# Packed attention and a gated feed-forward layer in one kernel: the first batch written out in another order

## The chip, the cores and the metric

The kernel runs on 1 core of one Trainium2 chip. The metric is the device time of one execution in microseconds (us); lower is better. The engines are TensorE (PE for its matmuls, PEld for its weight loads), VectorE (DVE), ScalarE (ACT), GpSimd (POOL) and SyncE (SP), which issues nearly all DMA transfers.

## The reference, cut to what matters

Eight batches of 8 heads, 576 tokens and head dimension 64. In each head 32 packed queries `p` attend to `k` and `v`; what comes out serves as key and as value for an attention from `q`. The heads are laid side by side (512 wide) and go through a feed-forward layer with 2048 hidden columns. The weights are float64 in memory.

```python
def _attn_ref(q, k, v, p):
    ...
    p_packed = sm_attn(p, k, v)                 # 32 rows a head
    out = sm_attn(q, p_packed, p_packed)        # 576 rows a head
    return out.astype(np.float32)

def _moe_ref(x, w_in, w_out):
    h = x @ w_in                                # 512 -> 2048
    g = h * (1.0 / (1.0 + np.exp(-1.702 * h)))
    return (g @ w_out).astype(np.float32)       # 2048 -> 512
```

## The kernel before

All work is cut into small steps, each a Python function that issues a few instructions. A tuple called `order` lists 2856 steps in the sequence in which they are issued, and the schedule is manual: every engine, and every DMA queue, executes its own instructions strictly in the order in which the tuple issues them. The tuple therefore sets the order of every queue. A step's last argument may name the engine that does it (`dve`, `pool`); without one it takes the step's default.

The steps of one batch `b`, with the names that the profile shows:

- `load` issues the input transfers on SP: `k` (with `p` in front, tile `k`, in two parts), `v` (a large part 0 of 1024 KB, `v_last` as part 1 of 256 KB) and `q` in two parts. The three share two buffers, so `q` takes the buffer of `k`, and the next batch's `k` that of `v`.
- `scores1_first` / `scores1_mm` (L250) multiply packed queries with keys. In batch 0 `max1_first` (DVE L273), `bias1` (DVE L303) and `exp1_first` (ACT L314) follow, and `turn1_mm` (PE L345), `turn1_copy`, `turn1_last_copy` (ACT L364) bring the weights transposed into the tile `aT`. `pack` (PE L408) multiplies `aT` with `v`; `pack_end` (ACT L421), `pack_turn_mm` (PE L427) and `pack_turn_copy` give `PT`, the packed rows.
- In the other batches `exp1` (ACT L321) and `turn1_blocks` (DVE L376) take the place of the PE transposes. They write the tile `xb` (0 and 1 for the even and odd heads); eight transfers `turn1_out` (SP L384, `aside<-xb`) carry it to DRAM, and six `turn1_in` (SP L396, `aT<-aside`) bring it back into `aT`.
- `scores2_mm` (PE L495) multiplies `q` with `PT`. Then `scores2_turn` (DVE L506), `max2` (DVE L526), `sub2` (L530), `exp2` (ACT L534), `sum2` (DVE L539 to L541), `norm2` (POOL L545), `turn2` (DVE L551).
- Every large product works on values split into an upper and a lower part, which are multiplied as three matmuls. `a_upper`/`a_lower` split the attention weights, `m_upper`/`m_lower` (L471) the product `m` of `PT` with `w_in` that `m_chunk` (PE L437) makes 512 hidden columns at a time, `h_upper`/`h_lower` (L592) the gated values `ghi`/`glo`, `upper_w`/`lower_w` (L232) the weights `wo`. The upper part is a cast (L117 on ACT, L119 on DVE or POOL), the lower one a subtraction.
- `h_mm` (PE L605) makes 128 hidden columns of one half of the tokens, six matmuls. It writes one of two PSUM banks, so it must wait until the `h_mm` two before it has gone through `h_tanh` (ACT L613) and `h_gate`/`h_over` (DVE L595).
- `out_mm` (PE L665) adds 128 hidden columns to the output of 128 tokens, three matmuls of 128x512.
- In batch 0 the weights come in too. `load_w` (SP L189) brings tile number `n` of 32: 0 to 3 are `w_in` for the first 512 hidden columns, 4 to 7 four tiles of `w_out`, 8 to 11 `w_in` again, and so on. The tiles 0 to 3 are loaded and decoded in two halves of 256 columns. `begin_w` (ACT L208, `tops<-raw`) and `join_w` (DVE L220) decode the float64 words. Tiles 16 to 19 must be joined before `w_out` tiles 20 to 23 can be loaded, because these use the same memory.
- `warm` (PE L125) is a run of matmuls whose result nobody reads.

The casts that name no engine go to ACT, the subtractions that name none to POOL:

```python
    def upper_w(n, engine=nc.scalar):
    ...
    def h_upper(b, f, half, engine=nc.scalar):
    def h_lower(b, f, half, engine=nc.gpsimd):
```

Work of neighbouring batches is interleaved: while batch 0 is in its feed-forward layer, the keys, scores and transposes of batch 1 run in between.

Of the kernel before, what the change touches and what calls it, by code (L numbers as in the profile page):

```python
# [21 lines left out]
def kernel(  # L22
# [681 lines left out]
    early = [bank_acc(0), bank_acc(1)]  # L704
    late = [bank_acc(2), bank_acc(3)]
    inner = [bank_h, bank_h]
# [9 lines left out]
        (turn1_last_copy, 0), (sum1, 0, 1), (pack, 0, 0, late), (pack, 0, 1), (pack_end, 0),
        (pack_turn_mm, 0), (warm, 5, 2), (pack_turn_copy, 0, dve), (load_w, 2, 0), (begin_w, 2, 0),
        (join_w, 2, 0), (load, "q", 0, 0), (load, "q", 0, 1), (scores2_mm, 0, 0),
        (scores2_turn, 0, 0, 0), (scores2_turn, 0, 0, 1), (max2, 0, 0, 0), (max2, 0, 0, 1),
        (load_w, 3, 0), (begin_w, 3, 0), (warm, 6, 2), (sub2, 0, 0, 0, pool), (exp2, 0, 0, 0),  # L720
        (scores2_mm, 0, 1, late), (scores2_turn, 0, 1, 1), (scores2_turn, 0, 1, 0), (max2, 0, 1),
        (load_w, 1, 0), (warm, 9, 3), (warm, 10, 3), (join_w, 3, 0), (begin_w, 1, 0),
        (join_w, 1, 0), (sub2, 0, 0, 1, pool), (m_chunk, 0, 0, early, 0), (exp2, 0, 0, 1),
        (load_w, 0, 1), (begin_w, 0, 1), (sum2, 0, 0, 0), (norm2, 0, 0, 0, pool), (warm, 2, 3),
        (m_upper, 0, 0, 1, 0), (sub2, 0, 1, None), (exp2, 0, 1), (sum2, 0, 0, 1),
        (norm2, 0, 0, 1, pool), (sum2, 0, 1), (warm, 0, 3), (load_w, 3, 1), (begin_w, 3, 1),
        (join_w, 3, 1), (load, "k", 1, 0), (scores1_mm, 1, 0, inner), (turn2, 0, 0, 0),
        (turn2, 0, 0, 1), (scores1_copy, 1, 0, 1), (scores1_copy, 1, 0, 0), (warm, 3, 3),
        (m_upper, 0, 0, 0, 0), (m_lower, 0, 0, 0, 0), (load_w, 4), (begin_w, 4), (join_w, 4),
        (m_lower, 0, 0, 1, 0), (a_upper, 0, 0, 0), (a_upper, 0, 0, 1), (join_w, 0, 1),  # L730
        (load_w, 2, 1), (begin_w, 2, 1), (norm2, 0, 1, None, pool), (a_lower_mm, 0, 0, 0, bank_b),
        (a_lower_mm, 0, 0, 1, bank_b), (a_lower_copy, 0, 0, 1, dve), (turn2, 0, 1),
        (a_lower_copy, 0, 0, 0), (upper_w, 4), (join_w, 2, 1), (load_w, 1, 1), (begin_w, 1, 1),
        (join_w, 1, 1), (h_mm, 0, 0, 0), (h_tanh, 0, 0, 0), (h_gate, 0, 0, 0), (lower_w, 4),
        (load, "k", 1, 1), (a_upper, 0, 1, None), (a_lower, 0, 1),
        (scores1_mm, 1, 1, (bank_b, bank_b)), (scores1_copy, 1, 1, 0), (scores1_copy, 1, 1, 1),
        (scores1_max, 1, 0), (h_mm, 0, 1, 0), (h_tanh, 0, 1, 0), (h_gate, 0, 1, 0),
        (h_upper, 0, 0, 0), (h_lower, 0, 0, 0), (m_chunk, 0, 0, (bank_b, bank_b), 1),
        (m_upper, 0, 0, 0, 1, dve), (load_w, 5), (bias1, 1, 0), (begin_w, 5), (join_w, 5),
# [12 lines left out]
        (h_mm, 0, 3, 1), (h_tanh, 0, 3, 1), (h_over, 0, 3), (m_chunk, 0, 1), (h_gate, 0, 3, 1),
        (m_upper, 0, 1, 0, None), (m_lower, 0, 1, 0), (m_upper, 0, 1, 1, None), (m_lower, 0, 1, 1),
        (h_mm, 0, 3, 0), (h_tanh, 0, 3, 0), (h_gate, 0, 3, 0), (h_upper, 0, 3, 0, dve),
        (out_mm, 0, 1, 1), (load_w, 12), (load_w, 13), (scores1_max, 1, 1), (bias1, 1, 1),
        (load_w, 19), (begin_w, 12), (join_w, 12), (exp1, 1, 0), (lower_w, 6), (out_mm, 0, 2, 0),
        (h_lower, 0, 2, 1), (load_w, 14), (out_mm, 0, 2, 1), (h_upper, 0, 3, 1, dve),
# [12 lines left out]
        (h_mm, 0, 6, 0), (begin_w, 18), (h_tanh, 0, 6, 0), (h_gate, 0, 6, 0), (upper_w, 15),  # L770
        (lower_w, 15, dve), (out_mm, 0, 4, 1), (out_mm, 0, 5, 1), (turn1_out, 1, 1, 3),
        (begin_w, 17), (upper_w, 14), (join_w, 18), (join_w, 17), (turn1_out, 1, 1, 2),
        (h_mm, 0, 7, 1), (h_tanh, 0, 7, 1), (begin_w, 19), (join_w, 19), (out_mm, 0, 4, 2),
        (out_mm, 0, 5, 2), (h_over, 0, 7), (lower_w, 14, dve), (h_mm, 0, 7, 0), (h_tanh, 0, 7, 0),
        (h_gate, 0, 7, 0), (m_chunk, 0, 2), (h_gate, 0, 7, 1), (h_upper, 0, 6, 0),
# [6 lines left out]
        (load, "v", 1, 0), (upper_w, 21, dve), (join_w, 20), (upper_w, 20, dve),
        (lower_w, 21, dve), (h_upper, 0, 6, 1), (out_mm, 0, 6, 1), (h_lower, 0, 7, 1),
        (out_mm, 0, 7, 1), (h_mm, 0, 8, 0), (h_tanh, 0, 8, 0), (h_gate, 0, 8, 0),
        (h_lower, 0, 6, 1), (h_mm, 0, 8, 1), (turn1_in, 1, 1), (h_upper, 0, 8, 0),
# [659 lines left out]
```

## Time and profile before

| | before |
|---|---|
| median of 3 runs | 698.79 us (697.97 to 699.39) |
| the profiled execution | 699.15 us, span 697.4 us |
| PE busy | 685.8 us (98%) |
| DVE, ACT, POOL busy | 439.1, 258.3, 95.9 us |
| mean granted TensorE clock | 0.999 |
| first `h_mm` starts | 25.01 us |
| `pack` of batch 1 starts | 72.49 us |

Times inside the execution count from the start of the span. "Idle before, releaser" on a row is the time for which its engine waited just before it, and what let it go. Matmuls overlap, so the start of a matmul says more than its end.

### The profile page before, as it was taken

To read this page: it belongs to the slowest core of one execution; us is meant where nothing else is said; L and a number is where in the kernel's file an instruction comes from. 1 tells how busy PE (TensorE), PEld (TensorE's weight loads), DVE (VectorE), ACT (ScalarE), POOL (GpSimd) and SP (SyncE) were. 2 spreads that over 40 slices of the span, in tenths; PEclk is the share of its full clock that TensorE was granted. 3 is DMA by queue.
4 is the path that set the end of the run, shared out by engine and by line. 5 is a ranking of instruction groups with operands and counts; after the bars stand their busy time and mean duration, and the time that the engine had idled before them with its cause. 6 is when DMAs were issued, how large, how long until landed. Compare 5 with 4: busy or idle time off the path is not lost.

```text
span 697.4 us, 12984 instructions
## 1 busy us (share of the span) xinstructions
PE 685.8 (98%) x5030; PEld 560.8 (80%) x5030; DVE 439.1 (63%) x1111; ACT 258.3 (37%) x620; POOL 95.9 (14%) x115
## 2 busy tenths in 40 slices
PE   7999999999999999999999999999999999999997
PEld 5788688888888888887888878888888887878885
DVE  4987885537555467555685567775785647855453
ACT  3886544423324323433223233332232333333220
POOL 2553372122300224111000000000000000000000
PEclk9999999999999999999999999999999999999999
DMA  9989803342101612055000613034200160010001
GB/s 331 378 306 223 299 0 106 70 136 77 65 0 20 194 31 87 16 130 184 1 31 1 159 43 144 16 93 127 96 16 1 31 181 1 16 47 1 1 15 61
DMA packets 55260, 65.18 MB, mean 93 GB/s; under 512 B 35808, under 2 KB 40864, under 8 KB 54176
## 3 DMA queue, kind: packets, MB, share of 16 engines
q1 hardware_dynamic: 55120, 64.23, 29.1%
q8 instruction: 40, 0.66, 0.4%
q14 instruction: 20, 0.16, 0.1%
q10 hardware_dynamic: 80, 0.13, 0.0%
HBM read 50.78 MB, written 13.57 MB: 92 GB/s over the span
## 4 chain that ended last, share of the span: by engine, by line
PE 92%; DMA 4%; issue 1%; DVE 1%; SPq 1%; ACT 0%; DVEq 0%; ACTq 0%
PE acc L665 49%; PE h L605 28%; PE acc_over L665 5%; PE psm_None L437 4%; PE ps L495 1%; PE pspv L408 1%; PE ps L250 1%; DMA aT<-aside 1%; DMA q<-q 1%; DMA k<-pk 1%; DMA aside<-xb 1%; SPq L384 1%; SPq L396 0%; SPq L189 0%; DVE ghi L119 0%
## 5 line engine op out<-in xcount | busy, mean ns | idle before, releaser
L665 PE MATMUL acc<-wo,ghi 128*128 128x512 f32 x1024 | 322.9, 396 | 0.4 <-ACT ghi L117 0.4
L665 PEld LDWEIGHTS acc<-wo,ghi 128*128 128x128 f32 x1024 | 179.6, 188 | 41.0 <-issue 11.2
L613 ACT ACTIVATE g<-h 128x288 f32<-128x288 f32 x256 | 104.0, 410 | 276.8 <-PE h L605 261.3
L665 PE MATMUL acc<-wo,glo 128*128 128x512 f32 x512 | 201.9, 394 | 0.3 <-POOL glo L592 0.3
L595 DVE SCALAR_TENSOR_TENSOR g<-g,h 128x288 f32<-128x288 f32 (+1 forms) x256 | 104.9, 415 | 116.2 <-ACT g L613 115.6
L605 PE MATMUL h<-ahi,mhi 128*128 128x288 f32 x496 | 139.9, 297 | 0.3 <-DVE g L595 0.3
L605 PE MATMUL h<-ahi,mlo 128*128 128x288 f32 x496 | 138.7, 295 | 0.0
L665 PEld LDWEIGHTS acc<-wo,glo 128*128 128x128 f32 x512 | 96.1, 188 | 23.6 <-POOL glo L592 0.9
L605 PEld LDWEIGHTS h<-ahi,mhi 128*128 128x128 f32 x496 | 93.2, 188 | 16.3 <-DVE x L506 4.9
L605 PE MATMUL h<-alo,mhi 128*128 128x288 f32 x496 | 104.9, 292 | 0.0
L605 PEld LDWEIGHTS h<-ahi,mlo 128*128 128x128 f32 x496 | 93.4, 188 | 6.9
L592 DVE TENSOR_TENSOR glo<-g,ghi 128x224 fp32r<-128x224 f32 (+1 forms) x183 | 76.2, 427 | 14.8 <-ACT ghi L117 10.8
L592 POOL TENSOR_TENSOR glo<-g,ghi 128x224 fp32r<-128x224 f32 (+1 forms) x73 | 55.4, 765 | 193.3 <-DVE ghi L119 86.7
L605 PEld LDWEIGHTS h<-alo,mhi 128*128 128x128 f32 x496 | 79.7, 188 | 0.1
L117 ACT CAST ghi<-g 128x288 fp32r<-128x288 f32 (+1 forms) x142 | 55.2, 403 | 54.4 <-DVE g L595 47.7
L595 DVE SCALAR_TENSOR_TENSOR over<-g,h 128x64 f32<-128x64 f32 x128 | 27.0, 214 | 30.6 <-ACT g L613 30.1
L471 DVE TENSOR_TENSOR mlo<-psm_None,mhi 128x512 fp32r<-128x512 f32 x60 | 40.6, 684 | 5.1 <-ACT mhi L117 4.9
L119 DVE CAST ghi<-g 128x224 fp32r<-128x224 f32 (+1 forms) x114 | 35.9, 320 | 7.0 <-PE acc L665 1.4
L665 PE MATMUL acc_over<-wo,ghi_over 128*128 128x512 f32 x128 | 39.8, 392 | 0.0
L117 ACT CAST mhi<-psm_None 128x512 fp32r<-128x512 f32 x45 | 26.2, 584 | 29.3 <-PE psm_None L437 29.3
L437 PE MATMUL psm_None<-w_in,PT 64*32 64x512 f32 x496 | 33.4, 596 | 0.0
L665 PEld LDWEIGHTS acc_over<-wo,ghi_over 128*128 128x128 f32 x128 | 23.6, 188 | 4.8
(95 smaller groups left out, 476.1 us busy)
## 6 DMA issues: line engine op xcount, KB each, us to landing
q<-q SPq DMA_DIRECT2D x16, 576.0 KB, 5.7
v<-v SPq DMA_DIRECT2D x8, 1024.0 KB, 5.4
o<-o SPq DMA_DIRECT2D x32, 256.0 KB, 2.8
raw<-w_out SPq DMA_DIRECT2D x16, 511.8 KB, 7.2
raw<-w_in SPq DMA_DIRECT2D x12, 511.8 KB, 8.9
k<-pk SPq DMA_DIRECT2D x8, 640.0 KB, 4.0
k<-pk SPq DMA_DIRECT2D x8, 576.0 KB, 6.7
aside<-xb SPq DMA_DIRECT2D x56, 72.0 KB, 2.3
```

Of the source, the lines that this page charges most:

```text
L117: nc.scalar.copy(dst, src)
L119: engine.tensor_copy(dst, src)
L250: nc.tensor.matmul(bank[32 * j : 32 * j + 32, :NH], kq["p", b][rows(eo), j, :], kq["k", b][rows(eo), half, j, :], start=True, stop=True,)
L384: nc.sync.dma_start(d[:, :, NP * eo + j, :], src.rearrange("t (g n) -> t g n", n=NPK))
L408: nc.tensor.matmul(bank[32 * j : 32 * j + 32, e * D : (e + 1) * D], aT[:, c, e, 32 * j : 32 * j + 32], vt[:, c, e0 : e0 + D], start=(c == ...
L437: nc.tensor.matmul(banks[eo][32 * j : 32 * j + 32, columns(part)], PT[rows(eo), j, :], w_in_sb[fc][rows(eo), j, columns(part)], start=True ...
L471: nc.vector.tensor_tensor(lo, bank[:, at], hi.bitcast(F32), op=ALU.subtract)
L592: engine.tensor_tensor(lo, src, hi.bitcast(F32), op=ALU.subtract)
L595: nc.vector.scalar_tensor_tensor(dst, th, 1.0, h, op0=ALU.add, op1=ALU.mult)
L605: nc.tensor.matmul(h[:, :NH], m[eo][part][:, fo : fo + P], a[:, eo * NH : (eo + 1) * NH], start=(n == 0), stop=(n == len(terms) - 1),)
L613: nc.scalar.activation(g, st["h", b, f, half][:, :NH], AF.Tanh, scale=1.702)
L665: nc.tensor.matmul(acc, gp[:, at : at + P], wo[f][:, part, :], start=(start and i == 0), stop=(stop and i == 2),)
```

## The change

Only the tuple `order` changes. It holds the same 2856 steps, and from its step 331 on (a little before the second half of batch 0's `h_mm`s) it is the same as before. The first 330 steps stand in another sequence, and 30 of them name another engine. There are as many `warm` steps as before.

Casts and copies that go from DVE to ACT: `turn1_copy` of batch 0 (two), `pack_turn_copy`, `a_lower_copy` (one), `m_upper` (one), `h_upper` for hidden tile 3 (two) and 5 (one), `upper_w` 6 and 21. From ACT to DVE: `a_upper` (one), `h_upper` for tiles 0 (two), 1, 2, 4 and 7 (one each), `upper_w` 7, 12, 14 and 15. From DVE to POOL: `sub2` of the second half, `h_lower` for tile 2 (one), `lower_w` 14 and 15. From POOL to DVE: `lower_w` 4, 7 and 13, `h_lower` for tiles 2 and 4 (one each).

The start of the diff, and one later line of it:

```diff
-        (load, "k", 0, 0), (warm, 7, 7), (load, "k", 0, 1), (scores1_first, 0), (max1_first, 0, 0),
-        (scores1_first, 1), (max1_first, 0, 1), (bias1, 0, 0), (load_w, 0, 0), (max1_first, 1, 0),
...
+        (load, "k", 0, 0), (load, "k", 0, 1), (warm, 7, 7), (scores1_first, 0),
+        (max1_first, 0, 0), (load_w, 1, 0), (begin_w, 1, 0), (scores1_first, 1),
+        (max1_first, 1, 0), (max1_first, 0, 1), (bias1, 0, 0), (load_w, 0, 0), (begin_w, 0, 0),
...
+        (h_tanh, 0, 1, 0), (join_w, 4), (h_gate, 0, 0, 0), (h_upper, 0, 0, 0, dve),
```

Three places show what it does to the queues.

The first is the start of the program. SP's queue before (`raw` is a weight tile on its way, 1023 columns make a half tile; 128x2048 is the large part of `v`):

```order
L157 DMA k_96<-pk 128x1280
L157 DMA k_96<-pk 128x1152
L189 DMA raw_135<-w_in 128x1023
L151 DMA v_161<-v 128x2048
L153 DMA v_161<-v_last 128x512
L189 DMA raw_235<-w_in 128x1023
L157 DMA q_239<-q 128x1152 x2
```

and now:

```order
L157 DMA k_96<-pk 128x1280
L157 DMA k_96<-pk 128x1152
L189 DMA raw_122<-w_in 128x1023
L189 DMA raw_139<-w_in 128x1023
L153 DMA v_154<-v_last 128x512
L151 DMA v_154<-v 128x2048
L189 DMA raw_184<-w_in 128x1023
L189 DMA raw_240<-w_in 128x1023
L157 DMA q_242<-q 128x1152 x2
```

Two more half tiles stand ahead of `q`, one more ahead of `v`, and the large part of `v` comes behind the small one.

At the same place ACT's queue before:

```order
L314 ACTIVATE x_0_0_107,sm_0_0_145<-ps_0_0_0_109,nb_0_0_133 128x288
L314 ACTIVATE x_0_0_107,sm_0_0_145<-ps_0_0_1_122,nb_0_0_133 128x288
L314 ACTIVATE x_0_1_110,sm_0_1_158<-ps_0_1_0_112,nb_0_1_143 128x288
L314 ACTIVATE x_0_1_110,sm_0_1_158<-ps_0_1_1_123,nb_0_1_143 128x288
L208 CAST tops<-raw_135 128x256
L364 ACTIVATE aT<-pstl_175,mask 128x256
```

and now:

```order
L208 CAST tops<-raw_122 128x256
L208 CAST tops<-raw_139 128x256
L314 ACTIVATE x_0_0_107,sm_0_0_142<-ps_0_0_0_109,nb_0_0_137 128x288
L314 ACTIVATE x_0_0_107,sm_0_0_142<-ps_0_0_1_125,nb_0_0_137 128x288
L314 ACTIVATE x_0_1_110,sm_0_1_159<-ps_0_1_0_112,nb_0_1_156 128x288
L314 ACTIVATE x_0_1_110,sm_0_1_159<-ps_0_1_1_126,nb_0_1_156 128x288
L117 COPY aT<-pst_0_166 128x4x128
L117 COPY aT<-pst_1_172 128x4x128
L364 ACTIVATE aT<-pstl_179,mask 128x256
```

The first decode steps of two weight halves stand ahead of the exponentials now, and the two copies into `aT` have come over from DVE.

The second place is DVE at the first gated values of batch 0. Before:

```order
L595 SCALAR_TENSOR_TENSOR g_0_0_405<-g_0_0_405,h_0_0_398 128x288
L294 TENSOR_REDUCE mx_1_0_342<-x_1_0_341 128x1
L595 SCALAR_TENSOR_TENSOR g_0_1_434<-g_0_1_434,h_0_1_427 128x288
L119 CAST mhi_0_0_364<-psm_0_0_1_441 128x256
L305 TENSOR_SCALAR nb_1_0_454<-mx_1_0_342 128x1
L220 SCALAR_TENSOR_TENSOR dec<-raw_452,tops 128x512
```

and now:

```order
L595 SCALAR_TENSOR_TENSOR g_0_0_419<-g_0_0_419,h_0_0_403 128x288
L119 CAST ghi_0_435<-g_0_0_419 128x288
L595 SCALAR_TENSOR_TENSOR g_0_1_430<-g_0_1_430,h_0_1_421 128x288
L232 TENSOR_TENSOR wo_449<-dec,wo_449 128x512
L119 CAST ghi_1_455<-g_0_1_430 128x288
L471 TENSOR_TENSOR mlo_0_0_338<-psm_0_0_1_438,mhi_0_0_337 128x256
L220 SCALAR_TENSOR_TENSOR dec<-raw_391,tops 128x512
```

Casts to `ghi` and a subtraction for `wo` stand between the gates; a maximum for batch 1 has gone further back, and the cast to `mhi` has gone to ACT.

The third place is SP's queue where batch 1's transposed weights go out to `aside` and come back. Before:

```order
L384 DMA aside_752<-xb_0_737 576x1x32
L384 DMA aside_752<-xb_1_726 576x1x32 x2
L384 DMA aside_752<-xb_0_737 576x1x32
L384 DMA aside_752<-xb_1_726 576x1x32
L384 DMA aside_752<-xb_0_737 576x1x32 x2
L384 DMA aside_752<-xb_1_726 576x1x32
L189 DMA raw_882<-w_out 128x2047
L151 DMA v_891<-v 128x2048
L396 DMA aT<-aside_752 32x4x256
```

and now, from behind the first of these transfers on (`v` of batch 1 and that first one stand ahead of this):

```order
L189 DMA raw_769<-w_in 128x2047
L384 DMA aside_745<-xb_0_743 576x1x32
L384 DMA aside_745<-xb_1_764 576x1x32
L189 DMA raw_799<-w_out 128x2047
L384 DMA aside_745<-xb_0_743 576x1x32
L189 DMA raw_830<-w_in 128x2047
L189 DMA raw_847<-w_out 128x2047
L384 DMA aside_745<-xb_1_764 576x1x32
L384 DMA aside_745<-xb_0_743 576x1x32
L384 DMA aside_745<-xb_1_764 576x1x32 x2
L189 DMA raw_881<-w_in 128x2047
L396 DMA aT<-aside_745 32x4x256
```

Five weight tiles (25, 21, 24, 20 and 26) now stand among and behind the transfers to `aside`; four of the five were issued ahead of them before. `v` has gone ahead of them.

More of the change, by code (lines that the diff above doesn't have):

```diff
@@ L716 @@
[L716 to L739, printed above, removed]
@@ L752 @@
[L752 to L757, printed above, removed]
@@ L770 @@
[L770 to L775, printed above, removed]
@@ L782 @@
[L782 to L785, printed above, removed]
-        (h_lower, 0, 8, 0, dve), (h_tanh, 0, 8, 1), (lower_w, 20), (h_gate, 0, 8, 1),
-        (h_over, 0, 8), (begin_w, 25), (join_w, 25), (out_mm, 0, 6, 2), (out_mm, 0, 7, 2),
@@ new lines @@
+        (load, "v", 0, 1), (bias1, 0, 1), (join_w, 1, 0), (exp1_first, 1, 0), (exp1_first, 1, 1),
+        (sum1, 0, 1), (turn1_mm, 0, 0), (join_w, 0, 0), (turn1_mm, 0, 1), (turn1_copy, 0, 0),
+        (load, "v", 0, 0), (turn1_last_mm, 0), (turn1_copy, 0, 1), (turn1_last_copy, 0),
+        (load_w, 3, 0), (pack, 0, 0, late), (pack, 0, 1), (sum1, 0, 0), (pack_end, 0),
+        (pack_turn_mm, 0), (begin_w, 3, 0), (pack_turn_copy, 0), (load_w, 2, 0),
+        (load, "q", 0, 0), (join_w, 3, 0), (warm, 6, 2), (load, "q", 0, 1), (scores2_mm, 0, 0),
@@ new lines @@
+        (begin_w, 2, 0), (join_w, 2, 0), (scores2_turn, 0, 0, 0), (scores2_turn, 0, 0, 1),
+        (load, "k", 1, 0), (load_w, 3, 1), (warm, 8, 3), (max2, 0, 0, 0), (sub2, 0, 0, 0, pool),
+        (exp2, 0, 0, 0), (max2, 0, 0, 1), (scores2_mm, 0, 1, late), (scores2_turn, 0, 1, 0),
+        (scores2_turn, 0, 1, 1), (load, "k", 1, 1), (sub2, 0, 0, 1, pool), (warm, 3, 3),
+        (load_w, 2, 1), (load_w, 0, 1), (max2, 0, 1), (sub2, 0, 1, None, pool),
+        (scores1_mm, 1, 0, inner), (sum2, 0, 0, 0), (norm2, 0, 0, 0, pool), (exp2, 0, 0, 1),
@@ new lines @@
+        (sum2, 0, 0, 1), (begin_w, 3, 1), (scores1_copy, 1, 0, 0), (scores1_copy, 1, 0, 1),
+        (m_chunk, 0, 0, early, 0), (m_upper, 0, 0, 0, 0), (exp2, 0, 1), (join_w, 3, 1),
+        (warm, 0, 3), (norm2, 0, 0, 1, pool), (scores1_mm, 1, 1, (bank_b, bank_b)),
+        (m_lower, 0, 0, 0, 0), (load_w, 4), (m_upper, 0, 0, 1, 0), (scores1_copy, 1, 1, 1),
+        (turn2, 0, 0, 0), (a_upper, 0, 0, 0), (sum2, 0, 1), (scores1_copy, 1, 1, 0),
+        (begin_w, 2, 1), (warm, 4, 2), (norm2, 0, 1, None, pool), (begin_w, 0, 1), (load_w, 1, 1),
@@ new lines @@
+        (turn2, 0, 0, 1), (warm, 5, 2), (warm, 9, 3), (begin_w, 4), (load_w, 5),
+        (a_upper, 0, 0, 1, dve), (a_lower_mm, 0, 0, 0, bank_b), (a_lower_copy, 0, 0, 0),
+        (a_lower_mm, 0, 0, 1, bank_b), (a_lower_copy, 0, 0, 1), (m_lower, 0, 0, 1, 0),
+        (h_mm, 0, 0, 0), (join_w, 2, 1), (turn2, 0, 1), (begin_w, 1, 1), (load_w, 9),
+        (a_upper, 0, 1, None), (h_tanh, 0, 0, 0), (h_mm, 0, 1, 0), (join_w, 0, 1), (join_w, 1, 1),
+        (h_tanh, 0, 1, 0), (join_w, 4), (h_gate, 0, 0, 0), (h_upper, 0, 0, 0, dve),
@@ L873 @@
[L873 to L878 removed]
+        (h_gate, 1, 3, 0), (h_over, 1, 3), (h_gate, 1, 3, 1), (load, "v", 2, 0),
@@ new lines @@
+        (turn1_in, 3, 4), (turn1_in, 3, 5), (pack, 3), (h_mm, 2, 10, 0), (sum1, 3, 0),
+        (pack_end, 3), (pack_turn_mm, 3), (pack_turn_copy, 3, dve), (h_mm, 2, 9, 0),
+        (h_tanh, 2, 10, 0), (h_tanh, 2, 9, 0), (h_gate, 2, 9, 0), (h_gate, 2, 10, 0),
+        (out_mm, 2, 8, 1), (m_chunk, 2, 3), (m_upper, 2, 3, 0, None), (h_upper, 2, 9, 0),
+        (m_lower, 2, 3, 0), (h_upper, 2, 9, 1), (h_lower, 2, 9, 1), (load, "q", 3, 0),
+        (load, "q", 3, 1), (scores2_mm, 3, 0, inner), (scores2_turn, 3, 0, 0), (out_mm, 2, 7, 2),
@@ new lines @@
+        (h_upper, 2, 15, 1, dve), (h_lower, 2, 15, 1, dve), (out_mm, 2, 14, 2),
+        (out_mm, 2, 14, 3), (a_lower, 3, 1), (a_upper, 3, 0, None), (a_lower, 3, 0),
+        (h_mm, 3, 0, 1), (h_tanh, 3, 0, 1), (h_gate, 3, 0, 1), (h_mm, 3, 0, 0), (h_tanh, 3, 0, 0),
+        (h_gate, 3, 0, 0), (h_lower, 2, 15, 0), (out_mm, 2, 15, 1), (out_take, 2, 1, dve),
+        (h_upper, 3, 0, 0, dve), (h_over, 3, 0), (h_upper, 3, 0, 1), (out_mm, 2, 15, 0),
+        (m_chunk, 3, 1), (scores1_mm, 4, 0, inner), (h_lower, 3, 0, 0), (load, "v", 4, 1),
@@ new lines @@
+        (scores2_mm, 4, 0, inner), (scores2_turn, 4, 0, 0), (h_upper, 3, 8, 1),
+        (h_lower, 3, 8, 1), (store, 2, 3), (scores2_turn, 4, 0, 1), (max2, 4, 0), (m_chunk, 3, 3),
+        (m_upper, 3, 3, 0, None), (h_mm, 3, 10, 0), (h_tanh, 3, 10, 0),
+        (m_upper, 3, 3, 1, None, dve), (m_lower, 3, 3, 1), (out_mm, 3, 7, 0), (m_lower, 3, 3, 0),
+        (h_gate, 3, 10, 0), (h_upper, 3, 9, 1), (h_lower, 3, 9, 1, dve), (out_mm, 3, 8, 0),
+        (sub2, 4, 0, None, pool), (load, "q", 4, 1), (out_mm, 3, 7, 2), (out_mm, 3, 8, 2),
@@ new lines @@
+        (h_mm, 4, 9, 0), (h_tanh, 4, 9, 0), (h_gate, 4, 9, 0), (turn1_in, 5, 0), (sum1, 5, 0),
+        (turn1_in, 5, 4), (load, "v", 5, 1), (turn1_in, 5, 5), (pack, 5), (h_upper, 4, 8, 0, dve),
+        (h_lower, 4, 8, 0, dve), (h_upper, 4, 8, 1), (pack_end, 5), (out_mm, 4, 7, 3),
+        (pack_turn_mm, 5), (h_lower, 4, 8, 1, dve), (out_mm, 4, 8, 3), (pack_turn_copy, 5),
+        (scores2_mm, 5, 0, inner), (scores2_turn, 5, 0, 0), (scores2_turn, 5, 0, 1),
+        (m_chunk, 4, 3), (max2, 5, 0), (sub2, 5, 0, None), (h_mm, 4, 10, 1), (h_tanh, 4, 10, 1),
```

831 lines of the change are left out of this document (418 added, 413 removed).

## The prediction

> **What bounds the kernel now.** I read the busy time of each engine by stretches first, to find where TensorE waits at all. In a row stand the stretch, its length, then busy us and count of PE, PEld, DVE, ACT and POOL, the granted clock, the DMA share and GB/s.
>
> ```profile
> 25.00:30.00 5.00, 5.00 (x55) 3.48 (x54) 5.00 (x11) 4.77 (x13) 4.07 (x4) 1.00 1.03 408
> ...
> 73.00:100.00 27.00, 27.00 (x251) 21.58 (x240) 21.96 (x50) 13.85 (x32) 13.90 (x15) 1.00 0.42 163
> ...
> 600.00:690.00 90.00, 90.00 (x510) 76.12 (x509) 48.33 (x130) 24.03 (x58) 0.00 (x0) 1.00 0.07 24
> 690.00:697.40 7.40, 2.54 (x11) 1.71 (x10) 0.69 (x1) 0.00 (x0) 0.00 (x0) 0.92 0.13 35
> ```
>
> From 73 us to the tail PE is never idle, and nothing there is in the change. The change keeps every matmul, the unread ones too. So the end moves by what PE's waits before 73 us move, or by a new wait later. The view of PE's waits up to 73 us names the large ones (total, times, longest):
>
> ```profile
> PE warm L125 <- POOL ident masks.py:199: 1.4, 1, 1.4
> PE pspv L408 <- DMA aT<-aside: 0.9, 1, 0.9
> PE pst L345 <- ACT x L314: 0.7, 1, 0.7
> ```
>
> The first is the start itself and stays. The chain of work that ended last shows three transfers on the path (start, length):
>
> ```profile
> 7.27 7.10 DMA q<-q
> ...
> 55.09 4.02 DMA aside<-xb
> ...
> 63.67 8.47 DMA aT<-aside
> ```
>
> So three things count: how early `q` and `PT` let the second scores start, whether DVE keeps up (in the first stretch above it is busy all 5.00 us), and when batch 1's transposed weights are back in `aT`. I take the change in that order.
>
> **The start.** Issues, instructions with what ended the wait before them, and the time of the first half tile from issue to landing:
>
> ```profile
> 1.65 0.43 SPq L189 DMA_DIRECT2D raw<-w_in  x1
> ...
> 8.04 0.50 ACT L314 ACTIVATE x<-ps,nb 128x288 f32<-128x288 f32 x1 [5.61 <-DVE nb L303]
> ...
> 9.96 0.50 ACT L208 CAST tops<-raw 128x256 f16<-128x256 bf16 x1
> ...
> 11.28 1.59 PE L408 MATMUL pspv<-v,aT 128*32 128x64 f32 x80 [0.45 <-DMA v<-v]
> ...
> 14.50 0.72 PE L495 MATMUL ps<-q,PT 64*32 64x288 f32 x16 [0.43 <-DMA q<-q]
> ```
> ```profile
> raw<-w_in SPq DMA_DIRECT2D x1, 255.8 KB, 7.1
> ```
> ```profile
> 10.00:15.00 5.00, 3.64 (x108) 2.48 (x106) 2.43 (x8) 1.93 (x6) 0.00 (x0) 1.00 1.02 392
> ```
> ```profile
> L117 ACT CAST mhi<-psm_None 128x512 fp32r<-128x512 f32 x45 | 26.2, 584 | 29.3 <-PE psm_None L437 29.3
> ```
>
> The transfers move 392 GB/s with the DMA engines full, so a half tile (255.8 KB, 0.262 MB) costs 0.67 us to whatever stands behind it. Two more stand ahead of `q`: it comes 1.34 us later, and the second scores, which waited for it at 14.50, start at 15.84. ACT comes out nearly the same. Its first decode now waits for the first half tile, landing at 1.65 + 7.1 = 8.75, the second for the next at about 9.4; with its 0.50 the exponentials begin at 9.9 instead of 8.04. Four of them take until 9.96 before, so until 11.8 now; then ACT does the two copies into `aT` that DVE did beside it (584 ns each, by the nearest ACT row of that width) and the short last one, to about 13.4. `pack` waits for that instead of for `v` (two transfers of a quarter megabyte more ahead of its large part, 11.28 + 1.34 = 12.6), ends about 14.4 where it ended at 12.87, and `PT` is there at 15.5. So `q` decides: the second scores start 1.3 us late. Bounds: 1.0, should `q` land early because nothing is queued behind it until `pack` has freed `v`'s buffer, to 1.6 with ACT the later one. That PE is idle more here costs nothing by itself.
>
> **From the second scores to the first `h_mm`.** The rows of DVE's work that leaves this stretch, of PE, and of kinds that come to DVE:
>
> ```profile
> 18.31 0.75 DVE L220 SCALAR_TENSOR_TENSOR w_in<-raw,tops 128x256 uint32<-128x256 uint32 x2
> ...
> 19.79 0.70 DVE L530 TENSOR_TENSOR x<-x,mx 128x576 f32<-128x576 f32 x1
> ...
> 25.01 0.29 PE L605 MATMUL h<-ahi,mhi 128*128 128x288 f32 x1
> ...
> 26.05 0.71 PE L250 MATMUL ps<-k 64*32 64x288 f32 x16
> ...
> 28.88 0.41 DVE L119 CAST mhi<-psm 128x256 fp32r<-128x256 f32 x1
> ...
> 36.27 1.29 DVE L220 SCALAR_TENSOR_TENSOR w_in<-raw,tops 128x512 uint32<-128x512 uint32 x2
> ...
> 37.39 1.27 PE L437 MATMUL psm_None<-w_in,PT 64*32 64x512 f32 x16
> ...
> 40.99 0.31 DVE L119 CAST ghi<-g 128x288 fp32r<-128x288 f32 x1
> ...
> 42.46 1.52 POOL L232 TENSOR_TENSOR wo<-dec,wo 128x512 fp32r<-128x512 f32 x1 [0.19 <-ACT wo L117]
> ...
> 42.75 1.37 DVE L119 CAST ghi<-g 128x224 fp32r<-128x224 f32 x1
> ```
>
> All four half tiles are now joined ahead of the second scores, which takes the two joins of 0.75 out of DVE's full stretch, and `sub2` of the second half (0.70) is POOL's. That is 1.45 less on DVE. It does not all count, since `norm2` of the first half queues behind that `sub2` on POOL; I take 1.1. The first `h_mm` then starts at 25.01 + 1.3 - 1.1 = 25.2. Ahead of it PE has already done the scores of batch 1 that took 0.71 at 26.05. PE is 0.5 us ahead at this point, between 0 and 0.9.
>
> **DVE after that.** The next test is the second `m_chunk` (37.39), which needs the four joins that ended at 36.27 + 1.29 = 37.56 (its first matmuls need only the first of them). These rows have what is still missing:
>
> ```profile
> L595 DVE SCALAR_TENSOR_TENSOR g<-g,h 128x288 f32<-128x288 f32 (+1 forms) x256 | 104.9, 415 | 116.2 <-ACT g L613 115.6
> ...
> L232 DVE TENSOR_TENSOR wo<-dec,wo 128x512 fp32r<-128x512 f32 x5 | 4.0, 803 | 0.0
> ```
> ```profile
> 96.39 1.57 PE h L605 x12
> ```
>
> From the second scores to the last of these joins DVE gets four casts to `ghi` (0.31 each, 1.24), one subtraction of weights (0.80) and one more gate (0.42), and loses the 1.45 of above and a cast to `mhi` (0.41): +0.6. `a_upper` for `a_lower_copy` is a cast for a cast. With the 1.3 of the start the joins end at 39.5. PE gets there with one `h_mm` more done (six of twelve matmuls in 1.57, 0.79), at 37.39 + 0.79 - 0.5 = 37.7. It waits, and is about 1.3 us behind its old timing (38.2) afterwards. Bounds: 0.3, if DVE's own short waits close up, and 2.4, if one cast is held up by POOL: that of 42.75 took 1.37 beside a POOL subtraction and ended with it, where the one at 40.99 took 0.31. The casts that ACT loses and gains lie beside PE's work, ACT being less full than DVE, and I cost them at nothing; so do POOL's, as far as no cast waits for them.
>
> [...]
>
> **The reload of `aT`.** SP's issues, DVE's last joins of the next four tiles, PE's waits around `pack`, and the sizes:
>
> ```profile
> 50.31 5.41 SPq L384 DMA_DIRECT2D aside<-xb  x8
> ...
> 56.48 1.79 SPq L151 DMA_DIRECT2D v<-v  x1
> 59.30 0.33 SPq L396 DMA_DIRECT2D aT<-aside  x1
> ```
> ```profile
> 54.04 1.88 DVE L220 SCALAR_TENSOR_TENSOR w_in<-raw,tops 128x512 uint32<-128x512 uint32 x3
> ```
> ```profile
> 70.11 0.73 PE L665 MATMUL acc<-wo,ghi 128*128 128x512 f32 x2 [0.42 <-ACT ghi L117]
> ...
> 71.12 0.50 PE L665 MATMUL acc<-wo,glo 128*128 128x512 f32 x1 [0.28 <-POOL glo L592]
> ...
> 72.49 1.32 PE L408 MATMUL pspv<-v,aT 128*32 128x64 f32 x80 [0.87 <-DMA aT<-aside]
> ```
> ```profile
> v<-v SPq DMA_DIRECT2D x8, 1024.0 KB, 5.4
> ...
> raw<-w_out SPq DMA_DIRECT2D x16, 511.8 KB, 7.2
> ```
>
> SP is strictly in order. Before, eight transfers to `aside` go out in 5.41 us (0.68 each), then one tile and `v`, and the first load of `aT` at 59.30. Now tile 21 stands behind the third of them and uses memory that is free only when tiles 16 to 19 are joined, at 54.04 + 1.88 = 55.9 before. With DVE behind by about as much as it gains from doing less between, I keep 55.9. After it come five transfers to `aside` (3.4) and three tiles (0.4 each): the first load of `aT` goes out at 60.9 at the earliest. It also has to wait until `aside` has landed, behind three tiles of 511.8 KB (0.524 MB, 1.34 us each at 392 GB/s): up to 64. Middle 62.5, 3.2 later than before.
> Against that stands `v` (1024 KB, 2.7 us), which is long in; tile 26 (1.3) takes part of its place. Before, 72.49 - 59.30 = 13.2 us went by from the first load to `pack`; now 13.2 - 2.7 + 1.3 = 11.8. `pack` of batch 1 starts at 62.5 + 11.8 = 74.3 instead of 72.49: +1.8, between +0.2 and +3.3. PE would come to it at 72.49 less its three waits (0.42, 0.28, 0.87) plus the 1.3 of above, at 72.2, so the reload decides and PE's earlier losses go under in its wait.
>
> **Sum.** +1.8 us on the profiled execution (699.15, its 697.4 us of span and 1.75 around it) is 700.95. That execution lies 0.36 above the median of the runs shown, so the forecast is 698.79 + 1.8 = 700.6.
>
> **Rivals.** *The lateness is swallowed.* The reload ends when it did, because the lost `v` weighs as much as the tiles, and PE, 1.3 behind, uses up the waits of 0.42, 0.28 and 0.87. For it: these waits are real slack. Against it: five tiles now stand where one stood. `pack` starts at about 72.8: +0.3, 699.1.
> *Faster.* The early `v` frees the queue, the first load of `aT` goes out by 58.6, and DVE keeps up: PE keeps its 0.5 us and loses the three waits, 1.57. `pack` starts at 70.4, and the end comes 2.1 earlier, 696.7. For it: `v`'s 2.7 us. Against it: tile 21, which waits for DVE, stands ahead of five transfers. It decides at 70.4 - 11.8 = 58.6.
> *DVE is held up by POOL.* Eleven casts have come to DVE, and two that meet a POOL subtraction while DVE is behind add 2.1 (1.37 - 0.31 each). Tile 21 goes out as much later, and `aT` with it: 1.8 + 2.1, about 702.7. For it: the row 42.75. Against it: in most other places DVE's casts show their short time.
>
> **How the numbers follow.** Forecast 0.48 (of it 0.15 below the bound of slower), swallowed 0.17, faster 0.18, held up 0.17. A measurement of this kernel tells about 0.2%, 1.4 us, from no change. Slower: 0.33 + 0.17 = 0.50; within: 0.15 + 0.17 = 0.32; faster: 0.18. The range, 697.0 to 703.2, takes in the ends of the reload, most of the held-up case and part of the faster one. The forecast's own range is 699.0 to 702.1.
>
> **What would show it.** Right: the exponentials (L314) begin near 9.9, the second scores near 15.8, the first `h_mm` near 25.2, PE waits for joins (L220) near 38 to 39, the first `aT` load is issued after 60.9, and PE's longest wait in the execution is for `aT` at `pack`, some 2 us. Wrong: if `q` does not come later, if DVE shows idle time between 25 and 38 us, or if the wait for `aT` is shorter than 0.87.

## The result: 707.2 us, slower, and the profile after

The changed kernel takes 707.17 us (median, 706.10 to 708.72), the kernel before 699.09 in the runs beside it: a ratio of 1.012 (95% interval 1.0094 to 1.0145). The profiled execution took 707.99 us with a span of 706.2. The forecast was 700.6, with a range up to 703.2.

The same stretches as before, from the view by stretches (length; busy us and count of PE, PEld, DVE, ACT, POOL; granted clock, DMA share, GB/s), and one long stretch that holds all of the changed part:

```profile
25.00:30.00 5.00, 4.37 (x37) 3.19 (x38) 4.97 (x11) 4.20 (x10) 2.44 (x3) 1.00 1.02 414
73.00:100.00 27.00, 24.67 (x248) 19.31 (x248) 18.75 (x41) 12.71 (x30) 10.22 (x12) 0.94 0.70 233
600.00:690.00 90.00, 90.00 (x519) 76.63 (x519) 52.25 (x143) 27.43 (x66) 0.00 (x0) 1.00 0.05 17
15.00:62.00 47.00, 42.84 (x317) 29.78 (x317) 45.54 (x92) 30.41 (x68) 20.52 (x20) 1.00 0.76 272
```

The same long stretch of the kernel before:

```profile
15.00:62.00 47.00, 45.61 (x342) 35.49 (x335) 41.92 (x97) 36.61 (x81) 24.18 (x25) 1.00 0.88 314
```

Between 15 and 62 us DVE is busy 45.5 of 47 us and yet finishes five instructions fewer than before, in 3.6 us more. So its instructions are longer on average, 0.50 us against 0.43. Late in the program PE is never idle, as before. PE's waits (total, times, longest):

```profile
PE pspv L408 <- DMA aT<-aside: 2.3, 1, 2.3
PE h L605 <- DVE g L595: 1.7, 4, 0.8
...
PE ps L250 <- DMA k<-pk: 1.3, 2, 0.8
PE psm_None L437 <- DVE w_in L220: 0.7, 1, 0.7
```

PE waits for DVE in several places where it did not before, and the wait for `aT` has grown from 0.9 to 2.3 us. The chain that ended last, around `pack` of batch 1 (start, length):

```profile
57.69 2.42 DVE w_in L220 x2
60.11 0.31 DVE g L595
...
64.79 4.74 DMA aside<-xb
...
69.67 0.34 SPq L396
...
72.42 6.55 DMA aT<-aside
78.97 0.24 issue
79.21 2.36 PE pspv L408 x80
```

Two joins that had taken 0.68 us each before now take 2.42 together and end at 60.1; tile 21 goes out behind them, the transfers to `aside` behind that, and `pack` starts at 79.21 instead of 72.49: 6.7 us late. The last join for the second `m_chunk`, from DVE's rows, and the issue of tile 21, from SP's:

```profile
41.62 0.68 DVE L220 SCALAR_TENSOR_TENSOR w_in<-raw,tops 128x512 uint32<-128x512 uint32 x1
```
```profile
60.14 0.34 SPq L189 DMA_DIRECT2D raw<-w_out  x1
```

`pack` then takes 2.36 us where it took 1.32. The granted clock there, second by second (same columns as above):

```profile
78.00:79.00 1.00, 0.00 (x0) 0.00 (x0) 0.69 (x3) 0.58 (x3) 0.00 (x0) 0.99 1.04 364
79.00:80.00 1.00, 0.79 (x32) 0.82 (x36) 0.96 (x4) 0.43 (x1) 0.00 (x0) 0.50 0.96 361
80.00:81.00 1.00, 1.00 (x49) 1.00 (x44) 0.95 (x2) 0.00 (x0) 0.00 (x0) 0.50 1.01 412
81.00:82.00 1.00, 1.00 (x24) 0.83 (x15) 0.00 (x0) 0.59 (x3) 0.00 (x0) 0.50 0.91 362
82.00:83.00 1.00, 1.00 (x5) 0.77 (x4) 0.37 (x1) 1.00 (x2) 0.00 (x0) 0.80 0.07 29
```

PE runs at half clock for 3.4 us from the end of its wait on (78.98 to 82.40 us). By 85 us the kernel is 8.2 us late (`psm_None` at 85.51 against 77.33), at the end of the span 8.8.

One number sums up all kernels of this study: from the start of `pack` of batch 1 to the end of the span there are 625 us.

| kernel | median us | `pack` starts | span | span less `pack` |
|---|---|---|---|---|
| before | 698 to 699 | 72.5 | 697.4 | 624.9 |
| changed | 707.17 | 79.2 | 706.2 | 627.0, half clock |
| sequence only | 711.8 | 85.2 | 710.9 | 625.7 |
| engines only | 709.74 | 83.3 | 708.5 | 625.2 |
| casts back on ACT | 702.27 | 73.9 | 699.5 | 625.6 |
| POOL's splits on DVE | 704.9 | 76.7 | 703.8 | 627.1, half clock |
| tiles behind | 707.94 | 81.0 | 706.8 | 625.8 |
| tiles and decode behind | 711.08 | 83.9 | 709.3 | 625.4 |
| late fill | 712.65 | 84.6 | 711.0 | 626.4 |
| fill in the gap | 706.88 | 79.5 | 704.8 | 625.3 |
| changed start only | 701.06 | 71.6 | 696.6 | 625.0 |
| changed start, mended | 699.35 | 72.7 | 698.1 | 625.4 |
| start of before | 706.47 | 79.6 | 705.2 | 625.6 |
| early `v` | 698.94 | 71.0 | 695.8 | 624.8 |

Where no half clock falls between the start of `pack` and the last 3 us it is 624.8 to 625.8 (626.4 in one case). So the start of `pack` has to be explained, and the half clock. (Starts and spans are of the one profiled execution each.)

### The profile page after: what moved, and what is told of

It is laid out like the page before. It is cut to its first block, busy times and chain, and to the rows that moved or that the text cites. A ratio compares the mean times of both kernels' runs of the same rounds, so it can differ in the third digit from the quotient of the medians.

```text
span 706.2 us, 12979 instructions
## 1 busy us (share of the span) xinstructions
PE 691.9 (98%) x5030; PEld 563.6 (80%) x5030; DVE 444.5 (63%) x1113; ACT 258.1 (37%) x619; POOL 95.4 (14%) x114
## 4 chain that ended last, share of the span: by engine, by line
PE 89%; DVE 3%; DMA 3%; issue 2%; SPq 1%; ACT 1%; ACTq 0%; DVEq 0%
PE acc L665 48%; PE h L605 27%; PE acc_over L665 5%; PE psm_None L437 4%; PE pspv L408 2%; PE ps L495 1%; PE ps L250 1%; DMA aT<-aside 1%; DVE w_in L220 1%; DMA k<-pk 1%; DVE dec L220 1%; DMA raw<-w_in 1%; DMA aside<-xb 1%; DVE g L595 0%; SPq L384 0%
## 5 line engine op out<-in xcount | busy, mean ns | idle before, releaser
L592 DVE TENSOR_TENSOR glo<-g,ghi 128x288 fp32r<-128x288 f32 (+1 forms) x184 | 77.5, 432 | 15.0 <-ACT ghi L117 11.0
L592 POOL TENSOR_TENSOR glo<-g,ghi 128x288 fp32r<-128x288 f32 (+1 forms) x72 | 55.9, 782 | 200.1 <-DVE ghi L119 93.3
L117 ACT CAST ghi<-g 128x224 fp32r<-128x224 f32 (+1 forms) x139 | 54.1, 403 | 59.5 <-DVE g L595 52.8
L119 DVE CAST ghi<-g 128x288 fp32r<-128x288 f32 (+1 forms) x117 | 36.2, 315 | 6.9 <-PE acc L665 1.4
L437 PE MATMUL psm_None<-w_in,PT 64*32 64x512 f32 x496 | 36.1, 596 | 0.7 <-DVE w_in L220 0.7
L208 ACT CAST tops<-raw 128x512 f16<-128x512 bf16 (+1 forms) x36 | 24.7, 714 | 10.4 <-DMA raw<-w_in 6.0
```

What stands on the lines that cost most here:

```text
L117: nc.scalar.copy(dst, src)
L119: engine.tensor_copy(dst, src)
L208: nc.scalar.copy(top[n, part].bitcast(F16).rearrange("p (n h) -> p n h", h=2)[:, at, 1], raw[slot_of(queue[n])].bitcast(BF16).rearrange("p ...
L437: nc.tensor.matmul(banks[eo][32 * j : 32 * j + 32, columns(part)], PT[rows(eo), j, :], w_in_sb[fc][rows(eo), j, columns(part)], start=True ...
L592: engine.tensor_tensor(lo, src, hi.bitcast(F32), op=ALU.subtract)
```

## The experiments

The comparisons are with the kernel before, run beside each.

**Sequence or engines.** All 30 steps get their engine of before, in the new sequence; then the old sequence gets the new engines:

```diff
-        ..., (h_upper, 0, 0, 0, dve), ..., (lower_w, 14), ...
+        ..., (h_upper, 0, 0, 0), ..., (lower_w, 14, dve), ...
```

> The changed sequence with the engines of before for all 30 steps. If the sequence does the harm (late DVE joins and the transfers to `aside` among weight tiles), the time stays at 705 to 708 us, `pack` of batch 1 starts after 77 us and the first `aT` load goes out after 67. If the engines do it (casts on DVE that meet POOL's subtractions), the time goes back to 699 to 701 and `pack` starts at 72 to 74.

> The sequence of before with the changed kernel's engines for the 30 steps. The changed sequence with the engines of before took 711.8 us, 4.6 more than with its own. If the engines are good in themselves, this runs at 694 to 698, faster than before. If they only fit their own sequence, or put too many casts on DVE beside POOL, it runs at 700 to 706, and PE waits for DVE between 25 and 45 us.

The new sequence with the old engines took 711.8 us (ratio 1.0201, 1.017 to 1.0232), the old sequence with the new engines 709.74 (1.0156, 1.0128 to 1.0183). Each half alone costs 11 to 13 us, both together 8.1. Engines and sequence are fitted to each other: each costs more without the other than with it. Part of both losses is half clock, 10.2 and 6.8 us of it ahead of `pack` in the profiled executions. PE's largest waits show how such a misfit looks, first of the new sequence with the old engines:

```profile
PE h L605 <- POOL alo L574: 2.9, 1, 2.9
PE acc L665 <- POOL wo L232: 2.3, 2, 1.2
```

and of the old sequence with the new engines:

```profile
PE acc L665 <- DVE wo L232: 2.4, 1, 2.4
```

A split that lands on an engine whose queue is busy at that place makes PE wait 1.2 to 2.9 us there.

**The casts back on ACT.** The 11 casts that the change took from ACT are ACT's again:

```diff
-        ..., (h_upper, 0, 0, 0, dve), ..., (upper_w, 12, dve), ...
+        ..., (h_upper, 0, 0, 0), ..., (upper_w, 12), ...
```

> The changed kernel, but the 11 casts that it moved from ACT to DVE are ACT's again (ten casts that it moved the other way stay on ACT too). If DVE's lateness decides, DVE loses some 4 us of casts and up to 2 us of stretching beside POOL before 62 us: PE comes to `pack` 4 us earlier, and the end is at 701 to 703. If the order of the transfers decides, `pack` stays within 1.5 us of 79.2 and the time is 705.5 to 708. If ACT becomes the late engine instead, `h_mm` waits for ACT's tanh and the time is over 707.

702.27 us (ratio 1.0064, 1.0047 to 1.008): 3.8 us over the kernel before, where the changed kernel is 8.1 over it. Moving 11 casts takes back more than half. DVE over the same long stretch:

```profile
15.00:62.00 47.00, 43.37 (x333) 32.01 (x318) 40.08 (x87) 35.88 (x83) 23.78 (x23) 1.00 0.84 298
```

DVE has 5.5 us less to do than in the changed kernel, and ACT takes the casts without becoming late (up to 110 us no kind of PE's waits for ACT sums to over 0.4 us). The transfers are in the same order as in the changed kernel, but the first load of `aT` goes out at 65.5 instead of 69.7. DVE's lateness decides. How much of it is the casts' own length and how much is waiting beside POOL, this run does not separate.

**POOL's subtractions on DVE.** 16 subtractions of batch 0 go the other way, from POOL to the engine that is already full:

```diff
-        ..., (a_lower, 0, 1), ..., (h_lower, 0, 3, 0), ..., (lower_w, 12), ...
+        ..., (a_lower, 0, 1, dve), ..., (h_lower, 0, 3, 0, dve), ..., (lower_w, 12, dve), ...
```

> The changed kernel, but 16 subtractions of batch 0 (ten for `glo`, five for `wo`, one for `alo`) go from POOL to DVE, so that nothing of POOL's runs beside DVE between the first `h_mm` and `pack`. They are some 8.3 us more of DVE's own work (10 of 0.42, 5 of 0.68, one of 0.75). If DVE loses to POOL's overlap about what these subtractions last on DVE (the rows show 7.7 us of stretching between 15 and 62 us), the four joins of 0.69 keep that time each and the end stays within 1.5 us of 707.2. If the stretched rows have another cause than POOL, they stay stretched, DVE gets 8 us more work in a stretch that is full, and the time is 712 to 716.

704.9 us (ratio 1.0097, 1.0076 to 1.0119): not slower, though DVE has 16 instructions more. The median is 2.3 us under the changed kernel's, but the two intervals overlap. Its row for the long stretch:

```profile
15.00:62.00 47.00, 43.10 (x315) 31.66 (x316) 44.85 (x108) 31.88 (x71) 4.97 (x6) 1.00 0.81 288
```

DVE does 108 instructions in less busy time than the 92 of the changed kernel. The eight joins of 128x512 into `w_in` show why (minimum, median and maximum in ns), before, changed, and with the subtractions on DVE:

```profile
L220 DVE SCALAR_TENSOR_TENSOR w_in<-raw,tops x8: 678/686/693, 34.6 to 55.2; 128x512 uint32<-128x512 uint32 x8
```
```profile
L220 DVE SCALAR_TENSOR_TENSOR w_in<-raw,tops x8: 677/1286/1776, 37.5 to 58.8; 128x512 uint32<-128x512 uint32 x8
```
```profile
L220 DVE SCALAR_TENSOR_TENSOR w_in<-raw,tops x8: 677/680/689, 36.3 to 56.3; 128x512 uint32<-128x512 uint32 x8
```

In the changed kernel the joins run beside POOL's subtractions. DVE and POOL at one such place:

```profile
38.28 2.99 DVE L220 SCALAR_TENSOR_TENSOR w_in<-raw,tops 128x512 uint32<-128x512 uint32 x2
```
```profile
38.11 0.91 POOL L592 TENSOR_TENSOR glo<-g,ghi 128x288 fp32r<-128x288 f32 x1 [1.75 <-ACT ghi L117]
38.99 1.73 POOL L232 TENSOR_TENSOR wo<-dec,wo 128x512 fp32r<-128x512 f32 x1
```

POOL's second subtraction ends at 40.72, the second join at 41.27, 0.55 us later. The first join ends at 39.58, again 0.55 behind POOL's first (39.03), and so do three more, which started at 54.55, 57.61 and 58.83. Each of the five started while POOL's subtraction ran and ended as if it had waited for POOL's end, with 0.55 of its 0.68 us still to run. With the subtractions as its own work DVE stays full (44.85 of 47 us), and `pack` still starts 4.2 us later than in the kernel before.

**The order of the transfers.** Tiles 21, 24 and 20 go behind the eighth transfer to `aside`, and the decode of tile 21 behind its load; in a second version the decode and split steps of tiles 21 and 20 move back further, by up to some 40 steps:

```diff
-        ..., (load_w, 21), ..., (load_w, 24), ..., (load_w, 20), (turn1_out, 1, 1, 3), ...
+        ..., (turn1_out, 1, 1, 0), (load_w, 21), (load_w, 24), (load_w, 20), (load_w, 26), ...
```

> The changed kernel, but the weight tiles 21, 24 and 20 are issued behind the eighth transfer to `aside` instead of among them; the decode steps of tile 21 follow its load. If the order of the transfers decides, the first `aT` load goes out 4 us or more earlier than 69.7, PE's wait of 2.3 us at `pack` goes, the half clock behind it (about 1.5 us) with it, and the time is 702 to 704. If DVE's lateness decides, PE itself comes to `pack` only at about 76.9 and the gain is at most these 2.3 + 1.5; the transfers would then give back less than 2 us, with `pack` at 77.5 or later and the time 704.5 to 707.

> As the earlier run with tiles 21, 24 and 20 behind the eighth transfer to `aside`, but the decode and split steps of tiles 21 and 20 also stand later (ahead of the load of tile 23), so that ACT doesn't stand at tile 21 while casts to `ghi` queue behind it. If the order of the transfers held up the reload, all loads of `aT` go out 3 us or more earlier, PE doesn't wait at `pack` (it comes there at about 76.9), the half clock goes, and the time is 703 to 705. If the reload is bound by what the DMA engines have to move, `pack` stays at 79 or later and the time is over 706.

707.94 us (ratio 1.0133, 1.0118 to 1.0148) and 711.08 (1.019, 1.0166 to 1.0213): no gain, and a loss. The first load of `aT` did go out 4.6 us earlier, at 65.10. But the last one went out at 73.0 (73.4 before the move), the four between them going out over 3.99 us instead of 1.84, and PE got a new wait:

```profile
PE acc L665 <- ACT ghi L117: 2.4, 1, 2.4
```

ACT stood 2.7 us at the decode of a `w_out` tile that now came late, and casts to `ghi` queued behind it. In the second version that wait was 3.2 us, again with decodes (L208) on ACT right ahead of it; it was not followed further. The reload itself gained little: its last load landed at 79.53 us, in the second version at 78.66, in the changed kernel at 79.55, where the DMA engines are 97% busy from 70 to 79 us. So the place of these three tiles is worth at most 0.9 us to the reload, and the decode that waits for them costs more.

**The half clock.** 16 matmuls that nobody reads are put in front of `pack`, first as a step of the existing kind, then 8 in the PSUM bank that `pack` itself uses:

```diff
+        (warm, 11, 16), (pack, 1), ...
```
```diff
+        for _ in range(8 if b == 1 else 0):
+            nc.tensor.matmul(banks[0][:, :P], ident, ident, start=True, stop=True)
```

> The changed kernel with 16 more matmuls whose result nobody reads, right ahead of `pack` of batch 1, where PE stood idle from 76.9 to 79.2 us (12 of them took 1.60 us elsewhere, so 16 take about 2.1). If the half clock of 3.4 us behind that wait is caused by the wait, it goes: `pack` takes 1.3 instead of 2.4 us, the mean clock is 1.00 and the time 705 to 706, 1.5 us under the changed kernel's 707.2. If the half clock has another cause, it stays and the time is 707 to 708.

> The changed kernel with 8 more matmuls whose result nobody reads, written into the PSUM bank of `pack` of batch 1 right ahead of its own matmuls (about 2.1 us; the earlier fill stood in a bank that came free too late, so that it ran behind the wait and not in it). If the half clock of 3.4 us comes from PE's wait of 2.3 us, the wait for `aT` shrinks to some 0.3 us, `pack` takes 1.3 instead of 2.4 us, and the time is 705 to 706 in all runs. If the half clock has another cause, or matmuls in the gap only push `pack` back, the time is 707 to 709.

The first fill took 712.65 us (ratio 1.0204, 1.0176 to 1.0233), but its matmuls did not run in the gap:

```profile
79.39 5.26 PE L125 MATMUL warm<-ident 128*128 128x128 f32 x32 [2.58 <-DVE g L595]
```

The `warm` steps take one of the two banks of `h_mm`, so they had to wait for DVE's gate, ran behind the gap, and in part at half clock (a mean of 0.88 from 80 to 90 us); and one `warm` matmul makes two rows, so the 16 were 32. The second fill did what it should. The stretch of the gap and the one behind it:

```profile
76.90:79.20 2.30, 2.04 (x17) 1.80 (x16) 0.67 (x2) 1.34 (x3) 0.64 (x1) 1.00 1.08 299
79.20:82.60 3.40, 3.11 (x89) 2.70 (x90) 2.57 (x7) 2.27 (x6) 0.00 (x0) 1.00 0.89 356
```

`pack` starts at 79.49, as late as without the fill, but at full clock, and the span is 704.8 instead of 706.2. The half clock costs 1.4 us by these spans, 1.7 by the last column of the table (627.0 against 625.3). The median, 706.88 (706.22 to 707.68), is not clear of the changed kernel's: two of that kernel's four runs were at 706.1 and 706.4 with a mean clock of 1.000 and 0.998, the other two at 708.0 and 708.7 with 0.996. The half clock comes in some executions only, so the one execution with the gap filled does not show by itself that PE's idle time is the cause.

The traces of the changed kernel and of the kernel before say more. In the changed kernel full clock lasts from 10.72 to 78.98 us, half clock to 82.40, and full clock again to 703.62: 20, 1 and 182 times 3.413 us. In the kernel before full clock lasts from 6.68 to 696.18, 202 times that. Counted in stretches of that length, PE is busy for 1.31 us, or 38%, of the stretch just ahead of the piece at 78.98, and for 30% (0% in the kernel before) of the one ahead of the half clock at the end of the program. Every other stretch has 68% or more (73% in the kernel before), and full clock follows it. So in these two traces half clock follows a stretch in which PE stood idle for most of it. A wait of some 2 us may fill most of one stretch or be split over two; that this differs from one execution to the next is the author's guess and not shown, since one trace of each kernel was kept.

**Where in the program.** The sequences are joined at the first `h_mm`: the new start with the rest of before, and the other way round:

```diff
+        (load, "k", 0, 0), (load, "k", 0, 1), (warm, 7, 7), ...   # new, to the first h_mm
         (h_mm, 0, 0, 0), (h_tanh, 0, 0, 0), (h_gate, 0, 0, 0), ...   # before
```

> The changed kernel's steps up to its first `h_mm` (with their engines), and from there the sequence and the engines of before. If the start does no harm, as forecast (first `h_mm` near 25.2 to 25.5 with the scores of batch 1 already done), the time is 698 to 700. If the start leaves DVE behind (fewer joins are done at the first `h_mm`), the time is 701 to 704 and PE waits for joins near 38.

> The steps of before up to the first `h_mm`, and from there the changed sequence and engines. If the harm lies behind the first `h_mm` (DVE stretched beside POOL, and the late transposes for batch 1), the time is 704 to 708. If it lies in the start, the time is 698 to 701.

With the start of before the time is 706.47 us (ratio 1.0114, 1.0077 to 1.0151): nearly all of the loss lies behind the first `h_mm`. The new start alone gives 701.06 (1.0029, 1.0011 to 1.0047). Its profiled execution, at 698.37, is the shortest of its ten and no longer than the kernel before; the six longest (700.8 to 702.5) have a mean clock of 0.995 to 0.998, and no trace of them shows where. The one fault to be seen is two joins of 128x256 with PE's wait of 2.1 us on them:

```profile
26.21 2.88 DVE L220 SCALAR_TENSOR_TENSOR w_in<-raw,tops 128x256 uint32<-128x256 uint32 x2
```

The last test mends that one place, by taking two subtractions that run beside them from POOL:

```diff
-        ..., (lower_w, 4), ..., (a_lower, 0, 1), ...
+        ..., (a_lower, 0, 1, dve), ..., (h_gate, 0, 1, 0), (lower_w, 4, dve), ...
```

> The changed kernel's start with the rest of before, which took 701.1 us, with PE waiting 2.1 us for two joins of 128x256 that took 2.88 us together beside two of POOL's subtractions. Here these two subtractions (for `alo`, and for `wo` of tile 4, the latter behind the second gate) are DVE's. If the joins were stretched by POOL, they take 0.8 us, PE's wait falls under 0.8, and the time is 697 to 699, at or under before. If DVE is simply behind there, its 1.4 us more keep the time at 700.5 to 702.5.

```profile
27.04 0.72 DVE L220 SCALAR_TENSOR_TENSOR w_in<-raw,tops 128x256 uint32<-128x256 uint32 x2
```

The joins fall from 2.88 to 0.72 us and PE's wait for them is gone, so POOL had stretched them. The time is 699.35 us, but the ratio, 1.0024 (1.0011 to 1.0038), is not clear of the one without the mend, and still over 1: PE now waits 0.8 us for one of the two subtractions on DVE and 1.1 for `aT`. The wait was removed and others took its place.

**`v` early.** In the kernel before, `v` alone is moved:

```diff
+        ..., (load, "v", 1, 0), (turn1_out, 1, 0, 0), ...
-        ..., (join_w, 21), (load, "v", 1, 0), ...
```

> The kernel before, with the large part of batch 1's `v` issued ahead of the first transfer to `aside` instead of behind tile 21, and nothing else moved. By the prediction's term for `v` (2.7 us of transfer out of the 13.2 between the first load of `aT` and `pack`) the reload comes 2 to 3 us earlier; PE comes to `pack` at 71.6 at the earliest, so only its wait of 0.87 goes: 697.8 to 698.3, hardly to be told from before. If the early `v` only delays the transfers to `aside`, the time stays at 698.6 to 699.5.

698.94 us against 698.31 (ratio 1.0013, 0.9999 to 1.0027): no difference that can be told. In the profiled execution the first load of `aT` went out at 58.76, `pack` started at 71.0 without a wait for `aT`, and the span was 695.8: PE's wait went, as expected, but the median does not bear the gain out. And the reload came 1.3 us earlier (its fifth load landed at 70.80, before at 72.14), not 2 to 3. No version here beats the kernel before.

## Why the prediction was wrong

The place was right and the size was wrong. The longest wait in the execution is PE's for `aT` at `pack`, 2.3 us; DVE shows no idle time between 25 and 38 us; the first load of `aT` goes out after 60.9. All three had been named as signs. But a sign against the forecast was there too: `q` did not come later (its first part landed at 14.29 us, before at 14.37). By steps:

- *The start.* The exponentials began at 8.78 us (forecast 9.9), since the two half tiles had landed at 7.73 and 8.38 and not at 8.75 and 9.4, and the second scores at 14.99 (15.84), without a wait for `q`: they were 0.5 us late, not 1.34. So `q` did not decide, and two half tiles ahead of it did not delay it; why the first transfers were faster stays open. The first `h_mm` came at 25.47 (25.2), with the scores of batch 1 done. That this number held is luck: from the second scores to it 0.03 us were gained and not 1.1, which made up for the late start that did not come. On this stretch the cast to `ahi` that came to DVE, which the prediction counted as a cast for a cast, took 1.10 us (24.08 to 25.18) beside `norm2` on POOL (23.85 to 25.01).
- *DVE after that.* This is the step that failed. The joins of the second `m_chunk` were to end at 39.5 and ended at 42.30, and PE was to be 1.3 us behind, 2.4 at most; it came to `pack` at 76.9, where the forecast had 72.2. The prediction counted DVE's moved instructions by their undisturbed length (+0.6 us) and let one or two casts meet POOL at 1.06 each. The long stretch shows what was left out. The instructions beside a POOL subtraction, each less the median of its own form elsewhere, are 7.7 us too long between 15 and 62 us (3.0 in the kernel before), and 4.0 of these are on the eight joins, which the prediction took at 0.69. That joins could be held up at all was missing: it weighed only casts. From this mis-sized DVE term both follow: PE came to `pack` 4.7 us later than forecast, and tile 21 went out late.
- *What POOL held up.* Beside POOL, between 15 and 62 us of the changed kernel, joins took up to 2.6 times their length (1.78 us against 0.68), subtractions up to 2.4 (0.94 against 0.39) and a cast to `ghi` 3.4 (1.05 against 0.31), while the gates of 128x288 kept 0.44 to 0.46 and the reductions for the maxima 0.74 to 0.75. Why some kinds are held up and others are not, no run shows.
- *Tile 21.* "I keep 55.9" failed with it: the joins that it waits for ended at 60.11, and it went out at 60.14, 4.2 late.
- *From tile 21 to the first load of `aT`.* 6.6 was forecast, 5.0 to 8.1 at the bounds; it was 9.5. The load waited until `aside` had landed behind three tiles: the last transfer to it went out at 64.79 and landed at 69.53. The issue of tile 26 took 2.30 us, but it ended at 67.86 and held nothing up.
- *From that load to `pack`.* 11.8 forecast, 9.5 measured. The absence of `v` alone does not explain it: with `v` alone moved early, 12.3 us went by (58.76 to 71.04), against 13.2 before. Why it was 9.5 here stays open.
- *The sum.* 4.2 + 2.9 - 2.3 is 4.8 us more than the forecast's 1.8, 6.7 in all within the rounding of the steps. The half clock, 1.4 to 1.7 us in the executions that have it, was not foreseen, although the sum rested on a long wait of PE.

The rival with DVE held up by POOL, at 702.7 and with a chance of 0.17, was the mechanism, as the joins at 0.68 us without POOL beside them show. It was priced by two more collisions at one row of the kernel before. There were six more between 15 and 62 us (13 instructions over 1.25 times their usual length, 7 before), and on longer instructions. How few there were before did not say how many there would be once the queues were laid out anew: before, none of the eight joins took more than 0.69.

## What to carry to other kernels

When steps are moved, an engine's load is not the sum of its instructions' undisturbed lengths: lay the new order of DVE and POOL side by side and mark each pair of a kind that the traces show held up, here joins (1.78 us for 0.68) and subtractions as well as casts beside POOL's subtractions; where DVE is the full engine, a subtraction may be no dearer on DVE than beside it (704.9 us with 16 of them on DVE, 707.17 with them on POOL). Look for one event through which the lateness passes to the end (here the start of `pack`) and measure every variant by it. And a transfer that is moved back takes with it the in-order decode that waits for it, and everything queued behind that decode (here ACT stood 2.7 us and PE 2.4).
